# Retention and feed-forward on one core: weight loads paced by copies of h, ten blocks of h kept on chip, block 1 from step 16

## The chip, the cores and the metric

The kernel runs on one core of a Trainium2 chip. The metric is device time in microseconds of one execution. Beside the timed runs there is one profiled execution; all traces are of that one.

## The reference

The input is `q`, `k`, `v` of shape (8 batches, 8 heads, 576 positions, 64) in float32, and two weights, `w_in` (512 x 2048) and `w_out` (2048 x 512), in float64. The output is float32.

```
scores = (q @ k^T) / sqrt(64)
ret    = scores * gamma_head ** (i - j)   for i >= j, else 0
attn   = ret @ v
x      = attn, heads side by side: 4608 tokens x 512
h      = x @ w_in
g      = h - tanh(h)
out    = g @ w_out
```

## The kernel before, in words

**Tiles.** The sequence is cut into 9 chunks of 64 positions. One chunk of all 8 batches is a *block* of 512 tokens, and a block is the unit of the feed-forward part. The inner dimension 2048 is cut into 16 *weight blocks* f of 128. `mm1(n, f)` makes h for token block n and weight block f in one PSUM bank; `mm2(n, f)` adds g times weight block f of `w_out` to four PSUM banks. The precision of the two products is kept by splitting each operand into a high and a low word, so `mm1` and `mm2` are 3 x 4 matmuls of 128x512 each: high by high, high by low, low by high.

**Conversion of the weights.** Weights lie in DRAM as float64, two 32-bit words each. `load_w` issues one DMA of 512 KB on SyncE (SP) into the place where the converted block will stand. `guard` (two ScalarE instructions, lines 84 and 85) makes a mask of the raw block. `unit` converts a block to float32 words in three steps: VectorE line 93; VectorE line 98, with the guard of the next block ahead of it; VectorE line 100 and a ScalarE copy (line 103) that makes the high word. `finish` (VectorE line 110) makes the low word, one step into the next unit. `step()` takes one such step, `upto("load", n)` and `upto("guard", n)` go on in the stream of 32 blocks (16 of `w_in`, then 16 of `w_out` in the order 14, 15, 0 to 13).

**Attention.** The first chunk is taken apart for each of the 8 batches: scores (`s_first`), decay (`pm`, line 241), output (`own_first`), then `after_out` writes the high word of x on ScalarE (line 259) and the low word on VectorE (line 260). Later chunks go by pairs of batches (four pairs p a chunk; pairs 4 to 7 are chunk 1): `entry(p)` runs the scores of the next pair, the output of this pair and the new state as small matmuls, and then the mask, x, and the state. `load_pair` and `load_early` fetch a pair (1 MB); `scale_q` (VectorE) and `scale_v` (four ScalarE instructions, line 194) multiply it by the decay tables, `scale_k` (line 438) does so for keys of the first chunk.

**The first stage.** `seq` lists 32 calls of `mm1`: blocks 0 and 1 by all 16 weight blocks. The results are not taken through tanh at once: `mm1` copies h on ScalarE (line 309) into one of three buffers `g` and *spills* it to DRAM from SP (line 310). Only the last two go straight on. At fixed steps k the loop issues loads (`loads`), scalings (`scales`) and entries (`early`); block 1 needs all four entries.

**The second stage.** `late` lists 32 calls of `mm2`. The spilled h are fetched four steps ahead (`fetch`), taken through tanh (`resume`) and split (`words`). Weight blocks that are not converted yet are converted here, by `step()`.

**The rest.** For token blocks 2 to 8 `mm1` and `mm2` alternate, with an entry at every fourth step. The change leaves this part alone.

**Order.** `in_order` fixes that every engine runs its instructions in the order in which the code issues them, SP's and ScalarE's DMA queues too. A DMA on SP that has to wait holds up all DMAs behind it. Before the first matmul, `busy(WARM, P)` issues `WARM` matmuls on zeros, and each iteration of the first chunk issues one or two more.

**Places.** Tensors that live for a short time use the places of weight blocks that come late: tags `wo0` to `wo15`. The eight first tiles `a0` to `a7` stand in `wo15` to `wo8`, decay in `wo7`, the first query table in `wo6`, the key rows in `wo4` and `wo5`, and pairs 6 and 7 in `wo0` to `wo3`. PSUM has eight banks: `h` twice, `o0` to `o3`, `own`, `new`; in the first stage `mm1` goes round `h`, `o2`, `h`, `o3`, and uses only `h` in the last four steps.

Of the kernel before, what the change touches and what calls it, by code (L numbers as in the profile page):

```python
# [9 lines left out]
F32 = mybir.dt.float32  # L10
# [4 lines left out]
ALU = mybir.AluOpType  # L15
PSUM = bass.MemoryType.PSUM

B, H, S, D = 8, 8, 576, 64
NT, DM, DF = B * S, H * D, 2048
P = 128  # L20
NF = DF // P
NCC = DM // P
C = 64
NC = S // C
BLK = B * C
# [3 lines left out]


STEP = float(np.arctanh(0.5) / (1.06 * 2.0**-15))
WARM = 16

NP = NC * B // 2

# [20 lines left out]
        before[ins.engine] = ins.name  # L56


@with_exitstack
def retention_ffn(ctx: ExitStack, tc: tile.TileContext, ins, out, spill):  # L60
    nc = tc.nc
    first_d, krows_d, qkv_d, w_in, w_out, qtab_d, vtab_d, mask_d, decay_d = ins

    const = ctx.enter_context(tc.tile_pool(name="const", bufs=1))
    pool = ctx.enter_context(tc.tile_pool(name="pool", bufs=2))
    psp = ctx.enter_context(tc.tile_pool(name="psp", bufs=1, space=PSUM))
# [8 lines left out]
    def load_w(t, f):  # L75
        raw = const.tile([P, DM, 2], I32, tag=f"w{t}{f}", name=f"rw{t}{f}")
        src = w_in if t == "i" else w_out
        nc.sync.dma_start(raw.rearrange("p m t -> p (m t)"), src.bitcast(I32)[f])
        wraw[t, f] = raw

    def guard(t, f):
# [25 lines left out]
    def finish():  # L107
        while last:
            w, z = last.pop()
            nc.vector.tensor_tensor(w[:, 1], z.bitcast(F32), w[:, 0].bitcast(F32), op=ALU.subtract)  # L110
# [2 lines left out]
    turn = [NF - 2, NF - 1] + list(range(NF - 2))  # L113
    stream = [("i", f) for f in range(NF)] + [("o", f) for f in turn]
    at_ = {"load": 0, "guard": 0, "convert": 0}
    last, going = [], []

    def upto(what, n):
        while at_[what] < min(n, 2 * NF):
            {"load": load_w, "guard": guard}[what](*stream[at_[what]])  # L120
            at_[what] += 1

    def step():

        if not going:
            if at_["convert"] == 2 * NF:
                return finish()
            upto("guard", at_["convert"] + 1)
            going.append(unit(at_["convert"]))
            at_["convert"] += 1  # L130
        if next(going[0], "end") == "end":
            going.pop()

    def units(n):
        while at_["convert"] < min(n, 2 * NF) or going:
            step()
# [4 lines left out]
    def load_qtab(c):  # L141
        if c not in qtabs:
            if c == 1:
                qtabs[c] = const.tile([P, 4, C], F32, tag="wo6", name="qtab1")
            else:
                qtabs[c] = pool.tile([P, 4, C], F32, tag="qtab", bufs=1, name=f"qtab{c}")
            nc.sync.dma_start(qtabs[c], qtab_d[c - 1])

    def load_pair(p):
        if p >= NP:  # L150
            return
        c, pr = divmod(p, B // 2)
        load_qtab(c)
        a = pool.tile([P, 2, 4, 4, C], F32, tag="a", name=f"a{p}")
        nc.sync.dma_start(a, qkv_d[c - 1, 2 * pr : 2 * pr + 2].rearrange("u p t i s -> p u t i s"))
        loaded[2 * p], loaded[2 * p + 1] = a[:, 0], a[:, 1]
        loaded["pair", p] = a
        loaded["qv", p] = a[:, :, 0], a[:, :, 2]
# [15 lines left out]
    def load_early(p):  # L174
        c, pr = divmod(p, B // 2)
        if pr < 2:
            return load_pair(p)
        src = qkv_d[c - 1, 2 * pr : 2 * pr + 2].rearrange("u p t i s -> p u t i s")
        parts = []
        for t in range(2):  # L180
            parts.append(const.tile([P, 2, 2, 4, C], F32, tag=f"wo{2 * (pr - 2) + t}", name=f"a_early{p}_{t}"))
            nc.sync.dma_start(parts[t], src[:, :, 2 * t : 2 * t + 2])
        for u in range(2):
            loaded[2 * p + u] = Parts([part[:, u] for part in parts])
        loaded["qv", p] = parts[0][:, :, 0], parts[1][:, :, 0]
# [68 lines left out]
            xs[c0] = [pool.tile([P, NCC, BLK], F32R, tag=t, name=f"{t}{c0}") for t in ("xh", "xl")]  # L254
        return [x[:, :, b * C : (b + n) * C].rearrange("p i (u t) -> p u i t", u=n) for x in xs[c0]]

    def after_out(j, o, n):
        xh, xl = x_of(j, n)
        nc.scalar.copy(xh, o)
        nc.vector.tensor_tensor(xl, o, xh.bitcast(F32), op=ALU.subtract)  # L260

    def first_states(b, place):

# [29 lines left out]
            prep(p + 2)  # L293


    gs, ops = {}, {}

    def mm1(n, f, bank="h"):
        hp = psp.tile([P, BLK], F32, tag=bank, bufs=2 if bank == "h" else 1, name=f"h{n}_{f}")
        xh, xl = xs[n]  # L300
        k = 0
        for a, x in ((0, xh), (0, xl), (1, xh)):
            for cc in range(NCC):
                nc.tensor.matmul(hp, win[f][:, a, cc, :], x[:, cc, :], start=(k == 0), stop=(k == 3 * NCC - 1))  # L304
                k += 1
        g = pool.tile([P, BLK], F32, tag="g", bufs=3, name=f"g{n}_{f}")
        if n == 0 or n == 1 and f < NF - 2:

            nc.scalar.copy(g, hp)  # L309
            nc.sync.dma_start(spill[n, f], g)  # L310
        else:
            activate(n, f, hp, g)
# [72 lines left out]

    busy(WARM, P)

# [3 lines left out]
    def load_first(j, queue=nc.sync):  # L391
        loaded[j] = const.tile([P, 3, 4, C], F32, tag=f"wo{NF - 1 - j}", name=f"a{j}")
        queue.dma_start(loaded[j], first_d[j])

    load_first(0)
    load_first(1, nc.scalar)
    load_first(2)
    nc.scalar.dma_start(decay, decay_d)
    load_first(3)
    nc.scalar.activation(warm[:, :1], warm[:, :1], AF.Tanh)  # L400
    upto("load", 1)
    for j in range(4, B):
        load_first(j)
    upto("load", 2)
    nc.sync.dma_start(vtab, vtab_d)
    nc.sync.dma_start(krows[0], krows_d[0])
    upto("load", 3)
    load_early(B // 2)
    nc.sync.dma_start(mask, mask_d)
    upto("load", 4)  # L410

    firsts = {}

    def score_first(j):
        firsts[j] = psp.tile([P, 8, C], F32, tag=f"o{j % 2}", bufs=1, name=f"s_first{j}")[:, :4]
# [2 lines left out]
    run(score_first(0), [])  # L420
    after_score(0, firsts[0].unsqueeze(1), 1)
    for j in range(B):
        o = psp.tile([P, 8, C], F32, tag=f"o{2 + j % 2}", bufs=1, name=f"own_first{j}")[:, :4]
        run(score_first(j + 1) if j < B - 1 else [], m_out(j, o))
        if j < B - 1:
            after_score(j + 1, firsts[j + 1].unsqueeze(1), 1)
        busy(*((2, BLK) if j < 2 else (1, BLK // 2)))
        if j == 2:
            upto("guard", 1)
        after_out(j, o.unsqueeze(1), 1)  # L430
        if 3 <= j < 6:
            step()
    finish()
    units(2)

    def scale_k(t):
# [3 lines left out]
    def scores_of(k):  # L440

        return psp.tile([P, 2, 4, C], F32, tag=f"o{k % 2}", bufs=1, name=f"s{k}")

    lead = 13
    seq = [(0, f) for f in range(lead)]
    for f in range(lead, NF):
        seq += [(0, f), (1, f - lead)]
    seq += [(1, f) for f in range(NF - lead, NF)]  # L450
    late = [(1, f) for f in turn] + [(0, f) for f in range(NF)]
    early = {4: 4, 7: 5, 10: 6, 12: 7}

    loads = {0: (5, 5), 1: (6,), 3: (7, 6), 4: (8,), 5: (9,), 6: (10, 7), 7: (11,), 8: (12, 8)}
    scales = {1: 4, 3: 5, 6: 6, 9: 7, 11: 8}
    for k, (n, f) in enumerate(seq):
        last_two = k - (len(seq) - 2)
        if k > 8:
            upto("load", k + 5)
        if k in (1, 5):  # L460
            scale_k(k // 4)
        if k in early:
            scale_v(early[k])
        if last_two < 0:
            step()
        else:
            fetch(*late[2 + last_two])
        mm1(n, f, ("h", "o2", "h", "o3")[k % 4] if k < len(seq) - 4 else "h")
        if last_two < 0:
            step()  # L470
            if k < 24:
                step()
        if k in scales:
            scale_q(scales[k])
        if k in loads:
            upto("load", loads[k][0])
            for p in loads[k][1:]:
                load_early(p) if p < B else load_pair(p)
        if k == 2:
            nc.sync.dma_start(krows[1], krows_d[1])  # L480
            sc = scores_of(B // 2 - 1)
            ms, done = first_states(0, "new")
            run(m_score(B, sc[:, 0]) + m_score(B + 1, sc[:, 1]) + ms, [])
            after_score(B, sc, 2)
            done()
        if k in early:
            p = early[k]
            more = first_states(2 * (p - 3), f"o{(p + 1) % 2}") if p < B - 1 else None
            entry(p, scores_of(p), more)
        if k == 13:  # L490
            load_pair(B + 1)
        if k == 16:
            prep(B, False)
            prep(B + 1)
    p = B
    for k, (n, f) in enumerate(late):
        if 0 < k < len(late) - 1:
            words(*late[k + 1])
        if k < len(late) - 2:
            resume(*late[k + 2])  # L500
        if k + 4 < len(late):
            fetch(*late[k + 4])
        if k >= 1:
            step()
        if k in (3, 8, 13, 18):
            entry(p, psp.tile([P, 2, 4, C], F32, tag="h", bufs=2, name=f"s{n}_{f}"))
            p += 1
        if k < len(late) - 1:
            mm2(n, f)
# [70 lines left out]
```

## Time and profile before

| | |
|---|---|
| median of 3 runs | 918.22 us (917.11 to 919.02) |
| profiled execution | 916.44 us, of which the span from first to last instruction is 914.7 |
| TensorE busy | 884.2 us of the span |
| VectorE, ScalarE, GpSimd busy | 363.2, 288.1, 67.0 us |
| moved by DMA | 82.06 MB, mean 90 GB/s |
| mean granted TensorE clock | 0.989 |

Busy shares are means over the whole span; the first 150 us are another regime than the rest. In rows of windows the columns are: window, its length, then busy time and number of instructions of PE (matmuls), PEld (weight loads), DVE (VectorE), ACT (ScalarE) and POOL (GpSimd), then the granted TensorE clock as a share of full speed, the share of time the 16 DMA engines were busy, and GB/s. Rows of the chain of waits are: start, length, and what the chain goes through; "issue" is time in which an engine waited for nothing that the profile shows. Rows of a timeline are: start, duration, engine, line, operation, and in brackets the idle time before it and what ended it.

### The profile page before, as it was taken

How to read it: one execution, taken by the hardware profiler on the slowest of the kernel's cores; microseconds unless marked ns; L12 is line 12 of the kernel's file. 1: busy time of each engine (PE TensorE's matmuls, PEld its weight loads, DVE VectorE, ACT ScalarE, POOL GpSimd, SP SyncE). 2: the span in 40 equal slices, each digit the busy share in tenths (PEclk: the TensorE clock that was granted, in tenths of full speed). 3: DMA queues.
4: the chain of work that ended last, by engine and by line, in shares of the span. 5: the costliest groups of instructions: out<-in, count | busy, mean ns of one | idle time of the engine just before them, and what ended most of it. 6: DMA issues, size and time to landing. Idle time of an engine off the chain costs nothing.

```text
span 914.7 us, 17581 instructions
## 1 busy us (share of the span) xinstructions
PE 884.2 (97%) x7833; PEld 728.1 (80%) x7834; DVE 363.2 (40%) x548; ACT 288.1 (32%) x502; POOL 67.0 (7%) x59
## 2 busy tenths in 40 slices
PE   7957999999999999999999999999999999999997
PEld 5745888878888888888888888888888888888886
DVE  4645896765333323333333332334222332222222
ACT  3654785444322222222222222222221222222222
POOL 0000100111010111111101100001100111000000
PEclk9987999999999999999999999999999999999999
DMA  8745784554121113111311131112111221002001
GB/s 313 263 154 201 261 290 141 178 182 137 50 73 53 47 47 93 53 48 47 93 53 48 47 94 47 53 43 68 32 50 47 68 72 48 1 1 47 1 1 46
DMA packets 31356, 82.06 MB, mean 90 GB/s; under 512 B 3760, under 2 KB 4912, under 8 KB 31280
## 3 DMA queue, kind: packets, MB, share of 16 engines
q1 hardware_dynamic: 30672, 79.89, 26.7%
q8 instruction: 61, 1.00, 0.4%
q10 hardware_dynamic: 608, 1.05, 0.3%
q14 instruction: 15, 0.12, 0.0%
HBM read 63.62 MB, written 17.30 MB: 88 GB/s over the span
## 4 chain that ended last, share of the span: by engine, by line
PE 92%; DMA 3%; ACT 1%; DVE 1%; issue 1%; SPq 0%; ACTq 0%; DVEq 0%
PE o L356 43%; PE h L304 40%; DMA rwi<-in_w_in_dram 3%; PE s L233 3%; PE own L233 2%; PE new L233 2%; DMA decay<-in_decay_dram 1%; ACT mi L84 0%; PE own_first L233 0%; PE new_first L233 0%; ACT g L309 0%; DVE mi L93 0%; DVE ob L371 0%; DVE mi L100 0%; PE s_first L233 0%
## 5 line engine op out<-in xcount | busy, mean ns | idle before, releaser
L304 PE MATMUL h<-xh,wi 128*128 128x512 f32 x1152 | 308.4, 393 | 10.5 <-DVE wi L110 6.9
L356 PE MATMUL o<-wo,gh 128*128 128x512 f32 x1152 | 293.5, 393 | 0.4 <-DVE ob L371 0.4
L304 PEld LDWEIGHTS h<-xh,wi 128*128 128x128 f32 x1152 | 216.5, 189 | 58.6 <-DVE wi L110 8.2
L356 PEld LDWEIGHTS o<-wo,gh 128*128 128x128 f32 x1152 | 213.8, 188 | 46.9 <-DVE ob L371 1.6
L318 DVE TENSOR_TENSOR g<-h,g 128x512 f32<-128x512 f32 x114 | 78.8, 691 | 372.1 <-ACT g L317 372.1
L317 ACT ACTIVATE g<-h 128x512 f32<-128x512 f32 x114 | 68.2, 598 | 423.7 <-PE h L304 422.9
L356 PE MATMUL o<-wo,gl 128*128 128x512 f32 x576 | 158.3, 389 | 0.0
L304 PE MATMUL h<-xl,wi 128*128 128x512 f32 x576 | 154.7, 390 | 0.0
L304 PEld LDWEIGHTS h<-xl,wi 128*128 128x128 f32 x576 | 108.9, 189 | 23.0
L356 PEld LDWEIGHTS o<-wo,gl 128*128 128x128 f32 x576 | 108.1, 188 | 22.5
L320 DVE TENSOR_TENSOR gl<-g,gh 128x512 fp32r<-128x512 f32 x114 | 80.5, 706 | 78.2 <-ACT gh L319 71.3
L319 ACT CAST gh<-g 128x512 fp32r<-128x512 f32 x114 | 70.7, 620 | 87.9 <-DVE g L318 87.9
L167 POOL TENSOR_TENSOR a<-a,qtab 128x512 f32<-128x512 f32 x27 | 36.1, 1338 | 617.4 <-DMA a<-in_qkv_dram 546.4
L233 PE MATMUL own<-a,state 64*64 64x64 f32 x960 | 59.3, 221 | 0.0
L233 PE MATMUL own<-pm,a 64*64 64x64 f32 x960 | 57.9, 219 | 0.0
L233 PEld LDWEIGHTS own<-a,state 64*64 64x64 f32 x960 | 47.8, 134 | 0.4 <-issue 0.4
L233 PEld LDWEIGHTS own<-pm,a 64*64 64x64 f32 x960 | 48.0, 135 | 0.0
L233 PEld LDWEIGHTS s<-a 64*64 64x64 f32 x960 | 30.4, 134 | 10.6 <-issue 9.9
L168 POOL TENSOR_TENSOR a<-a,vtab 128x512 f32<-128x512 f32 x28 | 31.8, 1137 | 79.9 <-DMA rwi<-in_w_in_dram 79.9
L233 PE MATMUL s<-a 64*64 64x64 f32 x960 | 34.5, 221 | 0.0
L340 DVE TENSOR_TENSOR gl<-s,gh 128x512 fp32r<-128x512 f32 x30 | 22.9, 762 | 29.2 <-PE o L356 25.2
L339 ACT CAST gh<-s 128x512 fp32r<-128x512 f32 x30 | 18.7, 622 | 38.2 <-PE o L356 30.1
(57 smaller groups left out, 471.9 us busy)
## 6 DMA issues: line engine op xcount, KB each, us to landing
a<-in_qkv_dram SPq DMA_DIRECT2D x30, 1024.0 KB, 5.2
out_dram<-ob SPq DMA_DIRECT2D x68, 128.0 KB, 2.4
rwi<-in_w_in_dram SPq DMA_DIRECT2D x16, 512.0 KB, 4.9
rwo<-in_w_out_dram SPq DMA_DIRECT2D x16, 512.0 KB, 4.7
spill_dram<-g SPq DMA_DIRECT2D x30, 256.0 KB, 3.0
s<-spill_dram SPq DMA_DIRECT2D x30, 256.0 KB, 2.7
a<-in_first_dram SPq DMA_DIRECT2D x7, 384.0 KB, 6.4
a_early<-in_qkv_dram SPq DMA_DIRECT2D x4, 512.0 KB, 6.1
```

Of the source, the lines that this page charges most:

```text
L167: nc.gpsimd.tensor_tensor(a[:, :, 0], a[:, :, 0], table, op=ALU.mult)
L168: nc.gpsimd.tensor_tensor(a[:, :, 2], a[:, :, 2], vtab[:, c].unsqueeze(1).unsqueeze(3).broadcast_to([P, 2, 4, D]), op=ALU.mult)
L233: nc.tensor.matmul(out_, w, x, start=start, stop=stop)
L304: nc.tensor.matmul(hp, win[f][:, a, cc, :], x[:, cc, :], start=(k == 0), stop=(k == 3 * NCC - 1))
L317: nc.scalar.activation(g, h, AF.Tanh)
L318: nc.vector.tensor_tensor(g, h, g, op=ALU.subtract)
L319: nc.scalar.copy(gh, g)
L320: nc.vector.tensor_tensor(gl, g, gh.bitcast(F32), op=ALU.subtract)
L339: nc.scalar.copy(gh, g)
L340: nc.vector.tensor_tensor(gl, g, gh.bitcast(F32), op=ALU.subtract)
L356: nc.tensor.matmul(o[t], g[:, t * P : (t + 1) * P], wout[f][:, a, :], start=(f == first and k == 0), stop=(f == final and k == 2),)
```

## The change

1. `WARM` goes from 16 to 38.
2. `behind` adds a wait to the DMA just issued: in `load_w`, for pairs 6 and 7 and for the second key rows, SP waits until the latest copy of h (by its place in the code) is done. The list `pace` holds the names of these copies.
3. Ten results h of block 0 (f = 0, 1 and 5 to 12) are copied into *homes*, tiles in `wo7`, `wo13`, `wo12`, `wo11` and `wo10`, two to a tile, in place of `g`. They are spilled from there at steps 16 to 20, two a step. Six of block 0 and fourteen of block 1 are spilled as before.
4. The 32 calls go in plain order: block 0, then block 1 from step 16 (before: block 1 from step 14, alternating for six steps). Entries 4 to 7 stand at steps 4, 7, 10 and 13 (before 4, 7, 10 and 12).
5. Weight loads: blocks 0 to 4 and pairs 4 and 5 are issued before the loop, block k+5 after step k. Pairs 6 and 7 are issued at steps 2 and 5, pairs 8 and 9 at steps 9 and 14. The first weight block is issued ahead of the tiles of batches 2 to 7.
6. Conversion takes three steps a step of the loop up to step 15 (before: to step 23), then two; in the second stage two in the first four steps, then one.
7. In the first chunk block 0 is converted in iterations 1 to 3 (before 3 to 5), the outputs take turns in three PSUM banks in place of two, and the low words of batches 5 to 7 are made after the first weight block is finished. The first `mm1` takes the low words of x last.

```diff
-WARM = 16
+WARM = 38
...
+def behind(tc, name):
+    tc.add_manual_dep(
+        tc.nc.cur_bb.bb.instructions[-1], name,
+        mybir.DependencyInfo(mybir.DependencyClass.Sync, mybir.DependencyReason.DATA), reason="paced",
+    )
...
         nc.sync.dma_start(raw.rearrange("p m t -> p (m t)"), src.bitcast(I32)[f])
+        if pace:
+            behind(tc, pace[-1])
...
             nc.sync.dma_start(parts[t], src[:, :, 2 * t : 2 * t + 2])
+            behind(tc, pace[-1])
...
+    home = {0: 7, 1: 7, 5: 13, 6: 13, 7: 12, 8: 12, 9: 11, 10: 11, 11: 10, 12: 10}
...
-        for a, x in ((0, xh), (0, xl), (1, xh)):
+        for a, x in ((0, xh), (1, xh), (0, xl)) if n == f == 0 else ((0, xh), (0, xl), (1, xh)):
...
+        if n == 0 and f in home:
+            if home[f] not in homes:
+                homes[home[f]] = const.tile([P, 2, BLK], F32, tag=f"wo{home[f]}", name=f"home{home[f]}")
+            nc.scalar.copy(homes[home[f]][:, (f + 1) % 2 if f > 1 else f], hp)
+            pace.append(tc.nc.cur_bb.bb.instructions[-1].name)
+            return
...
             nc.scalar.copy(g, hp)
+            pace.append(tc.nc.cur_bb.bb.instructions[-1].name)
...
     load_first(0)
     load_first(1, nc.scalar)
-    load_first(2)
+    upto("load", 1)
     nc.scalar.dma_start(decay, decay_d)
-    load_first(3)
+    for j in range(2, B):
+        load_first(j)
     nc.scalar.activation(warm[:, :1], warm[:, :1], AF.Tanh)
-    upto("load", 1)
-    for j in range(4, B):
-        load_first(j)
-    upto("load", 2)
+    upto("load", 3)
     nc.sync.dma_start(vtab, vtab_d)
     nc.sync.dma_start(krows[0], krows_d[0])
-    upto("load", 3)
     load_early(B // 2)
     nc.sync.dma_start(mask, mask_d)
-    upto("load", 4)
+    upto("load", 5)
+    load_early(B // 2 + 1)
...
-        o = psp.tile([P, 8, C], F32, tag=f"o{2 + j % 2}", bufs=1, name=f"own_first{j}")[:, :4]
+        o = psp.tile([P, 8, C], F32, tag=("o2", "o3", "own")[j % 3], bufs=1, name=f"own_first{j}")[:, :4]
...
-        if j == 2:
+        low = after_out(j, o.unsqueeze(1), 1, j < 5)
+        if j >= 5:
+            lows.append(low)
+        if j == 0:
             upto("guard", 1)
-        after_out(j, o.unsqueeze(1), 1)
-        if 3 <= j < 6:
+        if 1 <= j < 4:
             step()
     finish()
+    for low in lows:
+        low()
     units(2)
...
-    lead = 13
-    seq = [(0, f) for f in range(lead)]
-    for f in range(lead, NF):
-        seq += [(0, f), (1, f - lead)]
-    seq += [(1, f) for f in range(NF - lead, NF)]
+    seq = [(n, f) for n in range(2) for f in range(NF)]
...
-    early = {4: 4, 7: 5, 10: 6, 12: 7}
-    loads = {0: (5, 5), 1: (6,), 3: (7, 6), 4: (8,), 5: (9,), 6: (10, 7), 7: (11,), 8: (12, 8)}
-    scales = {1: 4, 3: 5, 6: 6, 9: 7, 11: 8}
+    early = {4: 4, 7: 5, 10: 6, 13: 7}
+    scales = {1: 4, 3: 5, 6: 6, 9: 7, 12: 8}
...
-        if k > 8:
-            upto("load", k + 5)
...
-            if k < 24:
+            if k < NF:
                 step()
...
-        if k in loads:
-            upto("load", loads[k][0])
-            for p in loads[k][1:]:
-                load_early(p) if p < B else load_pair(p)
+        upto("load", k + 6)
+        if k in (2, 5):
+            load_early(B // 2 + 2 + (k - 2) // 3)
+        if k == 9:
+            load_pair(B)
+        for f in [f for f in home if home[f] == (7, 13, 12, 11, 10)[k - NF]] if NF <= k < NF + 5 else []:
+            nc.sync.dma_start(spill[0, f], homes[home[f]][:, (f + 1) % 2 if f > 1 else f])
         if k == 2:
             nc.sync.dma_start(krows[1], krows_d[1])
+            behind(tc, pace[-1])
...
-        if k == 13:
+        if k == 14:
             load_pair(B + 1)
-        if k == 16:
+        if k == NF:
...
-        if k >= 1:
+        for _ in range(2 if k < 4 else 1):
             step()
```

More of the change, by code (lines that the diff above doesn't have):

```diff
@@ L115, in retention_ffn @@
     at_ = {"load": 0, "guard": 0, "convert": 0}
-    last, going = [], []
+    last, going, pace = [], [], []
     def upto(what, n):
@@ L255, in x_of, with after_out @@
         return [x[:, :, b * C : (b + n) * C].rearrange("p i (u t) -> p u i t", u=n) for x in xs[c0]]
-    def after_out(j, o, n):
+    def after_out(j, o, n, low=True):
         xh, xl = x_of(j, n)
         nc.scalar.copy(xh, o)
-        nc.vector.tensor_tensor(xl, o, xh.bitcast(F32), op=ALU.subtract)
+        if low:
+            nc.vector.tensor_tensor(xl, o, xh.bitcast(F32), op=ALU.subtract)
+        return lambda: nc.vector.tensor_tensor(xl, o, xh.bitcast(F32), op=ALU.subtract)
     def first_states(b, place):
@@ L293, in entry @@
             prep(p + 2)
-    gs, ops = {}, {}
+    gs, ops, homes = {}, {}, {}
+    home = {0: 7, 1: 7, 5: 13, 6: 13, 7: 12, 8: 12, 9: 11, 10: 11, 11: 10, 12: 10}
     def mm1(n, f, bank="h"):
@@ L396, in retention_ffn @@
     load_first(1, nc.scalar)
-    load_first(2)
+    upto("load", 1)
     nc.scalar.dma_start(decay, decay_d)
-    load_first(3)
+    for j in range(2, B):
+        load_first(j)
     nc.scalar.activation(warm[:, :1], warm[:, :1], AF.Tanh)
-    upto("load", 1)
-    for j in range(4, B):
-        load_first(j)
-    upto("load", 2)
+    upto("load", 3)
     nc.sync.dma_start(vtab, vtab_d)
     nc.sync.dma_start(krows[0], krows_d[0])
-    upto("load", 3)
     load_early(B // 2)
     nc.sync.dma_start(mask, mask_d)
-    upto("load", 4)
-    firsts = {}
+    upto("load", 5)
+    load_early(B // 2 + 1)
+    firsts, lows = {}, []
     def score_first(j):
```

## The prediction

> **What bounds the kernel now.** I read the page's busy shares and slices first, then the windows, then the chain of waits and the engines' timelines for the first 150 us.
>
> ```profile
> span 914.7 us, 17581 instructions
> PE 884.2 (97%) x7833; PEld 728.1 (80%) x7834; DVE 363.2 (40%) x548; ACT 288.1 (32%) x502; POOL 67.0 (7%) x59
> PE   7957999999999999999999999999999999999997
> q8 instruction: 61, 1.00, 0.4%
> ```
>
> ```profile
> 30.00:97.00 67.00, 49.55 (x779) 39.63 (x776) 36.89 (x59) 35.04 (x71) 1.04 (x1) 0.87 0.58 197
> 97.00:148.00 51.00, 51.00 (x226) 42.20 (x226) 42.55 (x64) 38.28 (x67) 3.06 (x2) 1.00 0.80 277
> ```
>
> PE bounds the kernel everywhere except in the first four slices (23 us each). From 30 to 97 us it is busy 49.55 of 67 us at a mean granted clock of 0.87, while the DMA engines are only 58% busy. From 97 us on it never stops. What the change can win lies ahead of 97 us.
>
> The first product is 32 calls of mm1, four entries and a prelude at step 2. How long that would take without waiting follows from four rows: the first matmul of mm1, the first of mm2, eighteen undisturbed calls, and one entry of 128 small matmuls.
>
> ```profile
> 19.55 1.20 PE L304 MATMUL h<-xh,wi 128*128 128x512 f32 x4 [0.26 <-ACT xh L259]
> 148.61 1.98 PE L356 MATMUL o<-wo,gh 128*128 128x512 f32 x8
> 99.81 48.96 PE h L304 x216
> 156.80:160.00 3.20, 2.10 (x128) 1.96 (x128) 1.00 0.26 88
> ```
>
> One mm1 is 48.96/18 = 2.72 us, so 32 are 87.0. Entries 4 to 6 also make the first states (160 matmuls, 2.62 us each), entry 7 has 128 (2.10), the prelude 64 (1.05): 11.0. Work 98.0, time used 148.61 - 19.55 = 129.1, so **31.0 us are lost** in this stretch. That is the most the stretch can give.
>
> Where it goes, in the chain of waits:
>
> ```profile
> 28.38 0.33 SPq L310
> 28.75 4.53 DMA rwi<-in_w_in_dram
> 33.30 0.67 ACT mi L84
> 36.50 3.74 DMA rwi<-in_w_in_dram
> 42.48 5.01 DMA rwi<-in_w_in_dram
> 60.75 4.40 issue
> 73.29 8.33 DMA rwi<-in_w_in_dram
> ```
>
> ```profile
> 48.74 0.57 ACT L309 COPY g<-h 128x512 f32<-128x512 f32 x1
> 54.85 0.57 ACT L309 COPY g<-h 128x512 f32<-128x512 f32 x1
> 115.17 0.58 ACT L309 COPY g<-h 128x512 f32<-128x512 f32 x1
> 117.88 0.58 ACT L309 COPY g<-h 128x512 f32<-128x512 f32 x1
> ```
>
> A loop stands there: copy of h, its spill on SP, the weight load queued behind it, 4 to 5 us of transfer, the guard on ACT, and behind that guard, in ACT's order, the next copy. A step takes 6.1 us (48.74 to 54.85) where a fed one takes 2.71 (115.17 to 117.88). The 8.33 us is a load that the code issues behind a pair and another load. The 4.40 us named "issue" is something else (below).
>
> **The change, part by part.**
>
> *Position of the loads.* Step k guards block k+3. Before, that block is issued behind copy k-1, and from step 3 to 8 behind copy k itself, when its guard is due. After, load k+5 is issued behind copy k, so block k+3 is issued behind copy k-2: two steps ahead, 5.4 us at PE's pace. The new wait on SP names a copy that the spill ahead waited for anyway; it delays whatever follows in SP's queue only until that copy. Five blocks and pair 5 are issued before the loop; by the diff 8.7 MB in all. The rates are here:
>
> ```profile
> 8.00:12.00 4.00, 3.67 (x88) 2.23 (x81) 1.79 (x5) 1.66 (x4) 0.00 (x0) 1.00 1.03 402
> 30.00:34.00 4.00, 4.00 (x61) 3.49 (x58) 2.92 (x5) 1.36 (x4) 0.00 (x0) 1.00 0.97 335
> spill_dram<-g SPq DMA_DIRECT2D x30, 256.0 KB, 3.0
> rwi<-in_w_in_dram SPq DMA_DIRECT2D x16, 512.0 KB, 4.9
> ```
>
> At 402 GB/s from about 2.5 us, 8.7 MB are in by 24 us. The worst place later is step 2: spill 2, load 7, pair 6 and krows make 2.36 MB, 7 us at 335 GB/s; load 8, issued a step (3.2 us) later, then lands about 6.5 us after its issue, and is due after copy 5, two steps and an entry (8 us) later. The rest is looser: over steps 3 to 15 some 11.4 MB in 46 us, 250 GB/s. So I let no guard wait for a load.
>
> *What then is late next: DVE, ACT and PE, nearly level.* A conversion takes DVE 2.71 us in steady state:
>
> ```profile
> 114.52 0.69 DVE L93 SCALAR_TENSOR_TENSOR mo<-rwo,mo 128x512 int32<-128x512 int32 x1
> 117.23 0.68 DVE L93 SCALAR_TENSOR_TENSOR mo<-rwo,mo 128x512 int32<-128x512 int32 x1
> 26.17 1.71 ACT krows L438 x4
> 58.16 1.27 ACT L194 ACTIVATE a<-a,vtab 128x128 f32<-128x128 f32 x4
> ```
>
> That equals PE's 2.72; an entry adds 1.8 us to DVE (three operations of about 0.6) and 2.62 to PE, so PE still leads. Following the program by these durations: mm1 of step 1 waits for its high words as now (about 1.1 us); scaling krows (1.71) in front of copy 1 and the value scaling (1.27) that stands on ACT behind step 4's conversion make entry 4 start 2.75 us later than pure PE work would; entries 5 to 7 each wait about 0.5 for the value scaling. Together **4.25 us** (bounds 2 and 8).
>
> *Spills.* Ten of 256 KB leave steps 0 to 12 and go out, two a step, at steps 16 to 20, where a step also spills and loads: 1.31 MB a step, 6.55 MB in 13.6 us, of which 335 GB/s carry 4.6. With the 0.7 MB that steps 13 to 15 leave over (pair 9 falls there), the queue is 2.7 MB or 8.0 us late. Three g buffers cover three steps (8.2 us), four PSUM banks as much again; but the last four steps have two banks, and load 28 stands on SP until its home is spilled. I take **1.5 us** (0, if buffers cover all, to 8.0). The ten copies into homes replace ten copies into g: no cost.
>
> *Block 1 from step 16.* The same 32 calls in another order; weights 13 to 15 are needed one or two steps sooner, which the position of the loads covers. Fewer conversion steps after step 16 leave some 2.7 more blocks for mm2's stage; its first four steps convert twice: about 2.8 us of DVE against 2.72, and an entry at the fourth. **0.8 us** (0 to 2).
>
> *Warm-up, order of the first loads, low words.*
>
> ```profile
> 1.19 1.89 PE L384 MATMUL wps<-warm 128*128 128x128 bf16 x16 [1.19 <-DVE warm L378]
> 5.18 1.33 PE L233 MATMUL s_first<-a 64*64 64x64 f32 x20 [2.10 <-DMA a<-in_first_dram]
> 1.19 5.66 DMA decay<-in_decay_dram
> 10.48 0.09 PE s_first L233 x2
> 11.58 0.04 PE s_first L233 x2
> 16.98 0.42 DVE xl L260
> 17.41 0.60 DVE mi L100
> 18.39 0.70 PE own_first L233 x16
> ```
>
> 16 warm-up matmuls span 1.89 us, the last one's drain included, some 0.11 apiece; 38 end near 5.3 us, the scores start at 5.18 now, and the first mask waits for decay until 6.85 anyway, so they cost nothing. Pairs of small matmuls are 0.1 us apart until 11.2 us and 0.06 afterwards; if the clock rises earlier, two iterations shorten. Block 0's conversion moves to iterations 1 to 3, so the 0.60 us that held up the last mask goes, and three low words of 0.42 go behind. mm1 starts earlier by **1.1 us** (0 to 2.5). Weights ahead of a2 delay it by 1.3 us at 402 GB/s, to about 8 us, when iteration 1 begins: hidden.
> The Trainium skill, "TensorE: Matmul & The Clock Gate", Part 1, has the clock rise after one busy window of about 3.4 us that runs free of the kernel; by that 4.1 us of warm-up need not hold a whole window, and the gain would be 0.5 to 1.1 us by phase. That the trace shows a rise at 11.2 us agrees with either.
>
> *Instruction pages.* Nothing the profile shows ended the idle 4.40 us at 60.75 and this 0.61:
>
> ```profile
> 15.49 0.61 issue
> 65.15 1.78 PE new_first L233 x32
> q8 instruction: 1, 0.02, 3.1%
> ```
>
> The last row is the DMA between 62 and 64 us. On the whole page 61 such packets carry 1.00 MB, 16 KB each; PE's 15667 instructions make 257 a packet. Counted in the code, both stops come at a multiple of 256 instructions (about 62 and 76 further ones included): PE had used up a page. The page needed at 60.75 was asked for one page earlier, at the start of entry 5, and PE went on 6.8 us later, with the DMA queue full; the other took about 4.3. A page spent inside an entry lasts only 2.1 us, hence the stop. 22 more warm-up matmuls shift every boundary by 44 instructions: now boundaries fall early in mm1 of step 6 (5.2 us after the last) and at the start of mm1 of step 11 (3.1 us after the last, nearly all of entry 6). Against 4.3 to 6.8 us those stop 0 to 1.6 and 1.2 to 3.7. I take **3.0 us** (0 to 5.3); the old stops lie in the 31.0.
> The Trainium skill, "Runtime: NRT & Kernel Launch", Instruction fetch mechanics, calls the crossing of a 16 KiB boundary mostly hidden; by that the sum would be 3.0 us lower. The 4.40 us here says otherwise while the queue is full.
>
> **Sum.** 31.0 - 4.25 - 1.5 - 0.8 - 3.0 + 1.1 = 22.6 us. The profiled execution took 916.4 (span 914.7 and 1.7 around it): 916.4 - 22.6 = 893.8, so **894 us**. The median of the runs, 918.2, lies 1.8 higher.
>
> **Rivals.**
> 1. *Pages stop PE at every entry*: 4 x 4.4 = 17.6 in place of 3.0, about 908. For it: the queue will be fuller than today's 58%. Against: boundaries shift, and entries 4, 6 and 7 show no such stop now.
> 2. *The burst at steps 16 to 20 reaches PE in full*: 8.0 for 1.5, about 900. For it: the two banks of the last four steps. Against: today's 277 GB/s from 97 to 148 us with PE never idle.
> 3. *Nothing but PE work is left*: hand-offs, burst and pages cost nothing: 916.4 - 31.0 - 1.1, about 884.
> 4. *Slower: guards still find their load on the way*, so the loop stays and 16 steps are starved in place of 13: 3 x (6.1 - 2.7) = 10 more, about 926. It decides if a load takes over two steps (5.4 us) to land while steps run at PE's pace. For it: 8.33 us behind a pair. Against: 3.7 to 5.0 for the others.
> 5. *The loads gain nothing since something else holds the steps* (DVE and ACT handing each conversion over, never at 2.71 outside the fed stretch): no change, 917.
>
> **How the numbers follow.** A difference of 0.2% is about what can be told from none. Forecast 0.62 (its own range 888 to 900), rival 1 0.10, rival 2 0.13, rival 3 0.08, rival 4 0.04, rival 5 0.03. Faster 0.93, same 0.03, slower 0.04. The range 886 to 906 takes the forecast, rival 2, and part of 1 and 3.
>
> **What would show it.** Right: between 30 and 80 us PE near 100% at full clock, the chain there without weight loads, h copies 2.7 us apart (5.3 across an entry), mm2 starting near 126 us, the DMA above 80% from 20 us on. "issue" idle of 1 to 4 us near step 11 would show the pages; h copies waiting at steps 22 to 27 the burst. Wrong: ACT's guards still waiting for rwi, or long idle between an entry's small matmuls.

## The result, and the profile after

The changed kernel takes 896.42 us (median of 4 runs, 895.05 to 899.01), the kernel before 918.62 in the same comparison; the ratio is 0.9762, 95% interval 0.9735 to 0.9789. The forecast was 894 us, with a range of 886 to 906. The profiled execution took 896.47 us, 20.0 less than the one before; the medians differ by 22.2.

From the page of the changed kernel: span, busy times, and the slices of 22 us each.

```profile
span 894.7 us, 17603 instructions
PE 879.7 (98%) x7855; PEld 725.0 (81%) x7856; DVE 364.5 (41%) x548; ACT 287.3 (32%) x502; POOL 67.8 (8%) x59
PE   7989999999999999999999999999999999999997
DMA  9766943562311131102211131113111211002001
```

Of PE's first four slices (7, 9, 5, 7 before) the third and fourth now stand at 8 and 9; the 7 of the first is left. The windows say it in numbers (columns as before):

```profile
30.00:97.00 67.00, 64.69 (x862) 53.56 (x858) 56.57 (x87) 49.94 (x99) 4.30 (x3) 0.97 0.74 257
78.00:126.00 48.00, 48.00 (x213) 39.73 (x212) 34.03 (x50) 30.21 (x53) 3.26 (x2) 1.00 0.88 328
126.00:160.00 34.00, 32.44 (x375) 25.55 (x374) 29.18 (x45) 20.07 (x35) 3.24 (x2) 1.00 0.37 117
```

From 30 to 97 us PE is busy 64.69 of 67 us (49.55 before), at a clock of 0.97 (0.87), and DMA moves 257 GB/s (197). The stretch that the burst of spills was to burden, 78 to 126 us, has no idle PE at 328 GB/s. But behind 126 us PE, which did not wait at the start of this stage before, now idles 1.56 us.

First matmul of mm1, first of mm2, and PE's one long stop between them:

```profile
19.14 2.11 PE L319 MATMUL h<-xh,wi 128*128 128x512 f32 x8 [0.26 <-ACT xh L270]
66.22 1.65 PE L319 MATMUL h<-xl,wi 128*128 128x512 f32 x3 [2.31 <-issue]
126.23 1.98 PE L379 MATMUL o<-wo,gh 128*128 128x512 f32 x8
```

The first product takes 107.1 us in place of 129.1. The chain of waits inside it has no weight load any more; its long pieces are PE's own:

```profile
30.96 5.67 PE h L319 x24
39.60 8.50 PE h L319 x36
51.10 8.40 PE h L319 x36
63.91 2.31 issue
66.22 8.85 PE h L319 x31
77.20 46.49 PE h L319 x204
```

Three mm1 between two entries take 8.40 to 8.50 us where 8.16 is bare work. The stop of 2.31 us comes after five matmuls of mm1 in step 11, just behind entry 6: the place that the prediction's count of instruction pages had named, the start of that mm1. The 31 matmuls behind it take 8.85 us in place of 7.0, with the granted clock down to 0.59:

```profile
66.50:70.00 3.50, 3.50 (x10) 2.77 (x11) 0.45 (x1) 0.41 (x1) 1.04 (x1) 0.59 0.08 30
```

### The profile page after: what moved, and what is told of

Read it like the earlier page. It is cut to its first block, busy times and chain, and to the rows that moved or that the text cites. A ratio compares the mean times of both kernels' runs of the same rounds, so it can differ in the third digit from the quotient of the medians.

```text
span 894.7 us, 17603 instructions
## 1 busy us (share of the span) xinstructions
PE 879.7 (98%) x7855; PEld 725.0 (81%) x7856; DVE 364.5 (41%) x548; ACT 287.3 (32%) x502; POOL 67.8 (8%) x59
## 4 chain that ended last, share of the span: by engine, by line
PE 94%; DVE 2%; ACT 1%; issue 1%; DMA 1%; ACTq 0%; DVEq 0%
PE h L319 44%; PE o L379 42%; PE s L244 3%; PE own L244 2%; PE new L244 2%; DMA decay<-in_decay_dram 1%; DVE s L356 0%; PE new_first L244 0%; DVE gl L363 0%; PE own_first L244 0%; DVE ob L394 0%; DVE mo L110 0%; ACT wo L113 0%; ACT gh L362 0%; PE s_first L244 0%
```

## The experiments

The theory that came out of the prediction: what paid is that a weight block is issued two steps ahead of its guard; the homes and the added waits pay little by themselves; the largest stop left is an instruction page that comes late. Rivals: the spills taken out of the way did it, or the waits; and the stop has another cause. Comparisons below are with the medians 896.42 (changed) and about 918 (before, run beside each).

**Which part of the change pays**

*Loads alone, in the kernel before.*

```diff
-    upto("load", 4)
+    upto("load", 5)
+    load_early(B // 2 + 1)
...
-    loads = {0: (5, 5), 1: (6,), 3: (7, 6), 4: (8,), 5: (9,), 6: (10, 7), 7: (11,), 8: (12, 8)}
+    loads = {k: (k + 6,) for k in range(32)}
+    loads[2] += (6,)
+    loads[5] += (7,)
+    loads[8] += (8,)
...
-        if k > 8:
-            upto("load", k + 5)
```

> The kernel before with one part of the change: five weight blocks and pair 5 before the loop, block k+5 behind step k, pairs 6, 7 and 8 at steps 2, 5 and 8. No homes, no added waits, the old order of the 32 calls, 16 warm-up matmuls, old first chunk. Theory (the place of the loads is nearly the whole gain): 896 to 901, with a stop of about 3 us for a page near the end of entry 5. Rival (the plain order of the blocks or the homes are needed with it): over 906.

Measured 898.44 us, ratio 0.9786 [0.9767, 0.9806]: 19.7 of the 22.2 us with this part alone. mm2 starts at 130.55 us in place of 148.61. The forecast page stop is there too, at the end of entry 5:

```profile
54.73 1.97 PE L233 MATMUL new_first<-a,krows 64*64 64x64 f32 x32 [3.74 <-issue]
```

*The loads one step and two steps later, in the changed kernel* (two kernels).

```diff
-        upto("load", k + 6)
+        upto("load", k + 5)     # in the second kernel k + 4
```

> Every weight load in the loop is issued one step later (block k+4 behind copy k). Theory: copy, load (4.4 us), guard (1.3) and the next copy but one make a loop of some 6.6 us over two steps, 3.3 a step for 2.72 outside entries: 6 us slower, 900 to 906. Rival (the loads had room to spare): no change, 895 to 898.

> Every weight load in the loop is issued two steps later (block k+3 behind copy k), where the kernel before had it. Theory: the loop of 6.1 us a step is back, now for 16 steps, some 13 of them outside entries: 25 to 40 us more, 921 to 936, above the kernel before. Rival (homes and pacing carry the gain): under 910.

One step later: 902.45 us, 0.9826 [0.9807, 0.9845], 6.0 slower. Two steps later: 929.48 us, 1.0118 [1.0096, 1.0140], slower than the kernel before, with homes, waits and order all in place. The chain of this kernel shows the old loop again, and its copies of h in steps 3 and 4, on ScalarE, are 6.8 us apart:

```profile
29.33 3.97 DMA rwi<-in_w_in_dram
33.32 0.67 ACT mi L94
35.53 4.57 DMA rwi<-in_w_in_dram
40.12 0.68 ACT mi L94
49.04 3.53 DMA rwi<-in_w_in_dram
```

```profile
34.55 0.57 ACT L331 COPY g<-h 128x512 f32<-128x512 f32 x1
41.36 0.57 ACT L331 COPY g<-h 128x512 f32<-128x512 f32 x1
```

So two steps of lead are enough here, one costs 6 us, and none costs 33. This is the prediction's fourth rival as it would have come.

*No homes.*

```diff
-    home = {0: 7, 1: 7, 5: 13, 6: 13, 7: 12, 8: 12, 9: 11, 10: 11, 11: 10, 12: 10}
+    home = {}
```

> All sixteen h of block 0 are spilled at once through g; everything else as in the changed kernel (896.4 us). Theory (the place of the loads made the gain, the DMA has room): ten more spills of 256 KB in steps 0 to 12 make 14 MB in 46 us, 304 GB/s, just below the 335 measured; 896 to 901. Rival (taking the spills out of the way made the gain): over 906, with guards waiting for loads again.

Measured 897.82 us, 0.9776 [0.9753, 0.9799]: not told apart from the changed kernel, since the medians differ by 1.4 us, well inside the two intervals. Beside the added waits, no gain of the homes is shown.

*No added waits.* The three calls of `behind` are taken out; the order on SP stays.

```diff
-        if pace:
-            behind(tc, pace[-1])
...
-            behind(tc, pace[-1])     # pairs 6 and 7; second key rows
```

> The waits of loads for copies of h are taken out; the order on SP stays. Theory: loads come in time with or without the waits, so 895 to 899; only a stop of PE for an instruction page may last longer, since the queue is fuller. Rival (the waits keep transfers from colliding): over 902, with pair 6, the key rows or the pages late.

Measured 893.65 us, 0.9729 [0.9711, 0.9747], 2.8 below the changed kernel's median and below the range expected; the two intervals still overlap. The two profiled executions start mm1 at nearly the same time (19.14 us, and 19.07 without the waits), and the first product takes 103.69 us in place of 107.09. The trace tells why: PE has no stop in step 11. Window 62 to 66 us in the changed kernel, then without the waits:

```profile
62.00:66.00 4.00, 1.91 (x25) 1.26 (x19) 3.32 (x6) 1.59 (x4) 0.00 (x0) 1.00 0.78 291
```

```profile
62.00:66.00 4.00, 4.00 (x57) 3.42 (x48) 3.43 (x6) 1.66 (x4) 0.00 (x0) 1.00 0.02 4
```

Without waits the loads of steps 5 to 12 are all issued by 51 us and have landed before 62 (DMA share 0.02 in the window, 0.78 with them). The same page boundary finds an empty queue, and PE goes through.

**Whether the stop is an instruction page**

*33, 48 and 16 warm-up matmuls* in place of 38: the pages begin 10 instructions later in the program, 20 earlier, and 44 later; nothing else in the code changes.

```diff
-WARM = 38
+WARM = 33     # in the other two kernels 48 and 16
```

> 33 warm-up matmuls in place of 38: every instruction page of PE begins 10 instructions later in the program. Theory of the pages: the page that ended in step 11 now holds 26 instructions of mm1 beside 230 of entry 6, so 4.8 us pass from one boundary to the next in place of 3.1; the stop of 2.31 us shrinks to under 1, and PE's clock is not lowered after it: 892 to 895. Rival (the stop has another cause, or a fixed place): same stop at the same matmul, 896 to 897.

> 48 warm-up matmuls: pages begin 20 instructions earlier. Theory of the pages: one page lies wholly inside entry 6 (2.1 us) and nearly all of one inside entry 4 (3.4 us): a stop of 3 to 4 us within the last 20 instructions of entry 6 and one of about 2 after entry 4; 898 to 902. Rival: 896 to 897, the stop where it was.

With 33: 894.03 us, 0.9748 [0.9724, 0.9773]. With 48: 901.90, 0.9829 [0.9806, 0.9853]. The stops, first with 33 and then with 48:

```profile
66.28 1.67 PE L319 MATMUL h<-xh,wi 128*128 128x512 f32 x6 [1.09 <-issue]
```

```profile
42.47 1.15 PE L319 MATMUL h<-xl,wi 128*128 128x512 f32 x4 [2.19 <-issue]
69.20 0.38 PE L244 MATMUL new_first<-a,krows 64*64 64x64 f32 x5 [3.35 <-issue]
```

With 33 PE stops in the same mm1 after ten matmuls, 20 instructions with their weight loads, where with 38 it stopped after five, 10 instructions; and for 1.09 us in place of 2.31 (under 1 was expected). With 48 it stops inside the last matmuls of entry 6 and once more behind entry 4. Place and length go with the count of instructions; the code moves the same data. The medians of 33 and 38 alone would not tell them apart; 48 is clearly slower.

> 16 warm-up matmuls, as before the change: pages begin 44 instructions later. Theory of the pages: no stop in step 11, one of 3 to 4.5 us near the end of entry 5 (about 51 us) as the kernel before had it at 60.75; 895 to 900. The start of the first mm1 stays within 0.5 us of 19.14, since the granted clock rose at 11.2 and 11.6 us with 16 and with 38. Rival: the stop stays in step 11; or the start comes over 1 us later for want of warm-up.

Measured 898.74 us, 0.9800 [0.9775, 0.9826]. The stop is where the kernel before had it, at the end of entry 5, 2.89 us (3 to 4.5 were expected), and none stands in step 11:

```profile
54.31 1.88 PE L244 MATMUL new_first<-a,krows 64*64 64x64 f32 x32 [2.89 <-issue]
```

The first mm1 starts at 19.71, 0.57 later than with 38: the bound of 0.5 was just missed.

The counts agree across the kernels. In the order of the program, 985 matmuls lie ahead of the stop with 38 and with 33, and as many ahead of the one in entry 6 with 48; with 16, here and in the kernel before, it is 730. With their weight loads these are 1970 and 1460 instructions, two pages of 256 apart but for 2. The instruction queue (q8 in the DMA view) says the same: at each stop PE goes on 2.2 to 2.7 us after one of its packets has moved, at 63.5 us for the stop that ends at 66.22 in the changed kernel, at 62.8 for the one that ends at 65.15 in the kernel before.

*Worst position, empty queue*: no added waits and 48 warm-up matmuls.

```diff
-WARM = 38
+WARM = 48
...
-            behind(tc, pace[-1])     # all three
```

> Without the added waits and with 48 warm-up matmuls, the worst position of the pages. Theory (a stop needs both a page spent inside an entry and a full queue): after entry 4, about 40 us, the queue is full and the stop of 2 us stays; at entry 6 (58 to 66 us) the queue is empty without the waits, so the 3.35 us stop goes; 895 to 898. Rival (the position of the page alone decides): both stops stay, 899 to 902.

Measured 898.27 us, 0.9787 [0.9768, 0.9805], a little above the range, but the two stops went apart as expected:

```profile
42.70 1.63 PE L316 MATMUL h<-xl,wi 128*128 128x512 f32 x4 [2.45 <-issue]
67.15 0.38 PE L241 MATMUL new_first<-a,krows 64*64 64x64 f32 x5 [0.60 <-issue]
```

Behind entry 4 the queue is full and the stop stays (2.19, now 2.45); at entry 6 it is empty, and 3.35 us become 0.60. In these kernels a long stop takes both: a page spent nearly whole within an entry, and a full queue.

**The second stage, and a joined version**

*Single steps in the second stage.*

```diff
-        for _ in range(2 if k < 4 else 1):
-            step()
+        step()
```

> One conversion step a step in all of the second stage, in place of two in its first four. Theory: those double steps make VectorE late for the split of g there (2.4 us lost after 126 us against the kernel before); one step each is enough, the last block is converted by step 14 and needed at step 15: 894 to 895.5. Rival (the loss there has another cause, GpSimd's work beside VectorE's for one): 896 to 897.

Measured 893.32 us, 0.9727 [0.9705, 0.9750], just below the range; the interval overlaps the changed kernel's, so the traces have to decide. The first 51.8 us of mm2's stage, in the changed kernel and here:

```profile
126.23:178.00 51.77, 50.21 (x572) 40.26 (x571) 41.97 (x62) 28.64 (x50) 6.49 (x4) 1.00 0.43 141
```

```profile
127.99:179.80 51.81, 51.45 (x581) 41.96 (x579) 43.29 (x65) 29.94 (x53) 8.03 (x6) 1.00 0.47 149
```

PE's idle time falls from 1.56 to 0.36 us and nine more matmuls fit in. From the first matmul of mm2 to the end it is 766.3 us here and 768.5 in the changed kernel; all nine kernels with double steps stand between 768.4 and 769.2, the five with single steps, the kernel before among them, between 765.7 and 766.5. The double steps cost about 2 us and were not needed.

*Joined*: no added waits and single steps, both edited as above, and the third step of the first conversion in iteration 5.

```diff
-        if 1 <= j < 4:
+        if j in (1, 2, 5):
             step()
```

> The changed kernel without the added waits, with one conversion step a step in all of the second stage, and in the first chunk the third step of the first conversion in iteration 5 in place of 3 (there VectorE and ScalarE held up the mask of a later iteration; PE waited 1.8 us). Theory: 893.65 without the waits, 2.2 less in the second stage, about 1 less at the start: 889.5 to 891.5. Rival (the start is set by the clock's phase or the tiles' arrival): 891.5 to 893.

Measured **890.05 us**, 0.9699 [0.9682, 0.9717], the fastest of all. mm2 starts at 121.76. What the edit in iteration 5 adds isn't shown: in this profile the clock stayed up once it had risen, as it did in two kernels with the old iteration (below), and their first mm1 starts at 17.86 and 17.90, here at 17.74.

*Joined, without homes*, edited on the joined version.

```diff
-    home = {0: 7, 1: 7, 5: 13, 6: 13, 7: 12, 8: 12, 9: 11, 10: 11, 11: 10, 12: 10}
+    home = {}
```

> The joined version (no added waits, single steps in the second stage, third step of the first conversion in iteration 5; 890.05 us) without homes: all of block 0's h are spilled at once, and so SP's queue is paced by the spills again. Theory (homes only matter by what they let pass ahead of entry 6; without them the queue is in use at 58 to 66 us and the page stop of 2 to 3 us in step 11 is back): 892 to 894.5. Rival (homes are worth nothing): 889.5 to 891.5.

Measured 895.28 us, 0.9746 [0.9722, 0.9771]: 5.2 us more, above the range. The stop in step 11 is back and longer than expected:

```profile
70.09 1.44 PE L316 MATMUL h<-xl,wi 128*128 128x512 f32 x3 [4.62 <-issue]
```

The DMA share from 62 to 66 us is 0.92 here and 0.02 in the joined version. The profiled execution is the slowest of five (892.97 to 899.12 us): its first mm1 also starts 1.7 us later, so its length is not due to the homes alone. The comparison rests on the two medians, whose intervals do not overlap.

So homes do pay once the waits are gone: with the spills off SP's queue, loads run ahead and the queue is empty when entry 6 asks for its page. With the waits the loads could not run ahead, and homes brought next to nothing.

## Why the prediction was right, point by point

The sum was 22.6 us; the medians give 22.2, the two profiled executions 20.0. That the medians come so close is in part luck: the terms, measured in the changed kernel's trace, add up to 19.9. Pages, second stage, start and hand-offs were about 4.0 us worse than forecast, the burst of spills 1.4 better, and the profiled execution of the kernel before was 2.2 us faster than its median.

| Term | Taken | Measured | From |
|---|---|---|---|
| lost before, that could be won | 31.0 | 31.0 | 129.1 - 98.0 |
| hand-offs up to entry 6 | 4.25 | 4.6 | entry 4 starts at 36.63, 2.84 after bare work; the two cycles to 62.54 are 0.72 and 0.66 longer than 10.78, entry 4 itself 0.35 |
| pages | 3.0 | 4.4 | 62.54 to 77.20 is 14.66 us; bare work 10.26 |
| burst of spills | 1.5 | 0.1 | 77.20 to 126.23 is 49.03 us; 18 mm1 are 48.96 |
| second stage | 0.8 | 2.4 | 894.7 - 126.23 against 914.7 - 148.61 |
| earlier start | 1.1 | 0.4 | 19.55 to 19.14 |

*Position of the loads.* Right, and now shown: the loads alone bring 19.7 us, and two steps later the gain turns into a loss. No guard waited for a `w_in` block in the changed kernel. One reading of the old order was off: block k+3 came behind copies k-1 and k only up to step 9; from step 10 on the old code (`upto("load", k + 5)` ahead of mm1) already issued it behind copy k-2.

*Spills.* Over-sized. The term let the queue carry 335 GB/s; from 88 to 114 us, with weight loads and spills mixed, it carried 406. By that rate the backlog is about 4.3 us and not 8.0 (an estimate from the same 6.55 and 0.7 MB). One copy of h waited for a spill:

```profile
107.68 0.59 ACT L331 COPY g<-h 128x512 f32<-128x512 f32 x1 [1.18 <-DMA spill_dram<-g]
```

PE had no idle time from 78 to 126 us, so buffers and PSUM banks covered what was late. Rival 2 counted on the low rate and left out this cover.

*Pages.* The place and the stop of 2.31 us (1.2 to 3.7 forecast) were right, and the mechanism is shown. What the term left out is the clock: after the stop PE ran at 0.59 for 3.5 us, which cost 1.8 us more. The stop of up to 1.6 us in step 6 didn't come. Rival 1 (a stop at every entry) is out: where a boundary falls decides.

*Second stage.* Right in kind (VectorE at 2.8 for 2.72 a step), off by three: the stage lost 2.4 us, not 0.8, and single steps gave 2.2 of them back.

*Start.* The step that failed outright is the one on the clock in the warm-up part: with more warm-up matmuls the clock was to rise earlier, and two iterations to shorten. It did rise earlier, but in the profiled execution it fell again. The first 20 score matmuls, the first output and the next warm-up matmuls, in the changed kernel and then in the kernel without homes (same code up to here):

```profile
5.26 0.80 PE L244 MATMUL s_first<-a 64*64 64x64 f32 x20 [0.20 <-DMA a<-in_first_dram]
7.82 0.29 PE L244 MATMUL own_first<-pm,a 64*64 64x64 f32 x2 [1.76 <-DVE pm L252]
9.20 0.63 PE L407 MATMUL wps<-warm 128*128 128x512 bf16 x1 [0.33 <-issue]
```

```profile
5.35 1.33 PE L244 MATMUL s_first<-a 64*64 64x64 f32 x20
7.61 0.27 PE L244 MATMUL own_first<-pm,a 64*64 64x64 f32 x2 [0.92 <-DVE pm L252]
8.22 0.61 PE L407 MATMUL wps<-warm 128*128 128x512 bf16 x2
```

In the changed kernel the 20 matmuls take 0.80 us in place of 1.33, so the clock is up by 5.3 us. PE is done sooner and waits longer, 1.76 us, for the mask that needs decay. The granted clock then falls to 0.50 at 7.95 us and is back at 11.36; in between one warm-up matmul of 512 columns takes 0.63 us, as long as two in the other kernel. There the clock rises a little later, PE waits 0.92 us, and the clock stays up. The first mm1 starts at 19.14 and at 17.86. Of the profiled executions with 33 or more warm-up matmuls, the six in which PE waited 1.76 us or more at this place all lost the clock, the five in which it waited 0.92 to 1.53 kept it. That the wait is the cause was not tested. With 16 warm-up matmuls the clock is still down at 8.75 us (the column of the granted clock shows 1.00 until its first fall, so a low clock before it has to be read from the matmuls):

```profile
8.75 1.04 PE L407 MATMUL wps<-warm 128*128 128x512 bf16 x2
```

The Trainium skill, "TensorE: Matmul & The Clock Gate", Part 1, has the clock follow a window of about 3.4 us that runs free of the kernel. The 3.41 us between fall and rise agree with that length.

*The added waits* were costed at nothing, as waits for a copy that the spill ahead waits for anyway. Ahead of the loads behind steps 5 to 12 there is no such spill: these copies go into homes. There the added wait alone holds the loads back, and so keeps the queue in use at 58 to 66 us, when the page is due. Taking the waits out gains 2.8 us by the medians and 3.4 in the first product of the two profiles.

## What to carry to other kernels

Where an engine's order couples a load, the work on it and the next evacuation, count how many steps ahead each load is issued against how long it takes to land: here one step of lead was worth 6 us and two 33. Don't pace loads for its own sake: a queue that is emptied early also serves the engine's instructions, and dense runs of small instructions (256 in 2 us) need them then. And when a stop has no releaser in the trace, count instructions from the start: stops that lie whole pages apart name it, and a few instructions more or less ahead of it move it.

## What was not expected of the hardware

A late instruction page stopped PE for 0.6 to 4.6 us. Behind every stop of 1.90 us or more the granted clock was lowered (behind the one of 2.31 us it was 0.59 for 3.5 us, and stop and clock together cost 4.1 us); behind those of 1.09 us and less it was not. At the start, a wait of 1.8 us right after the clock's rise went with a fall to 0.50 for 3.4 us, and executions of the same starting code differ by up to 1.3 us in the first mm1's start. And spills among the loads did not slow the 16 DMA engines: 406 GB/s from 88 to 114 us of the changed kernel, 402 GB/s with loads alone from 8 to 12 us of the kernel before.
